# First four tiles in streams of their own, first projections by tile, and two pairs of value products in column tiles

## The chip, the core and the metric

The kernel runs on one core of one Trainium2 chip. The metric is the device time in microseconds (us) of one execution, the median over several. The core has five engines with queues of their own: TensorE (PE) multiplies matrices and loads their stationary operand (PEld), VectorE (DVE) and ScalarE (ACT) work elementwise, GpSimd (POOL) does small things and masks, and SyncE (SP) issues the transfers (DMA). Each engine works its queue off in order; semaphores order the engines against each other.

## The reference

Two layers, each twice with the same weights: attention in four segments with a compressive memory, then a feed-forward block with ReLU. There are 2048 tokens of 640 features, 32 heads of 20, and 1728 hidden features.

```
for s in range(4):                                  # segments of 512 tokens
    p = softmax(q_s k_s^T * scale + causal mask)
    a_dot = p v_s
    a_mem = phi(q_s) M / (phi(q_s) z + 1e-6)
    o_s = g * a_mem + (1 - g) * a_dot               # g = sigmoid(beta)
    M += phi(k_s)^T v_s;  z += sum(phi(k_s))
x = x + (o @ wo);   x = x + relu(layernorm(x) @ w1) @ w2
```

with q, k, v = layernorm(x) @ wq, wk, wv. All inputs are bf16. In the first segment the memory is empty, so only the softmax part counts there.

## The kernel before

Everything stays on chip; x is held in 16 tiles of 128 tokens (`x_sb`). The two attention layers have four segments each. A segment's heads go in 8 groups of four heads, and two groups make a pair m, 32 pairs over the two layers; pairs 0 to 3 are the first segment of the first layer.

The order of the instructions is made by a planner (`Sched`, lines 173 to 374). Each part of the work is a generator, a stream with a priority (`S.add`, from line 1480 on), that yields operations with assumed durations, waits for events (`Need`) and for buffers (`Acq`). The planner always emits the operation that can start first, with the priority deciding ties, and so writes a fixed queue for every engine. Where it foresees a gap of over 300 ns on PE it fills it with small products on a unit matrix (`keep_busy`, line 189; they show as L627). The whole is planned once for each of 32 values of an assumed cost of a change between PE's tile modes (`STARTS`, line 161), and the plan with the smallest end, by the planner's own estimate with random transfer delays, is the one that is built.

PE has three modes here. Full products use all of the 128 x 128 array. The scores (L1103) run four at a time on 20 rows each, one for each head, in row mode. Products of the probabilities with the values (L1246) run four at a time on 32 columns each, in column mode.

The opening: x tiles 0 and 1 are loaded by transfers of their own (`x0a`, `x0b`), tiles 2 and 3 by one (`x01`). Two streams normalize them, `first_ln_a` for tiles 0 and 1 and `first_ln_b` for 2 and 3. DVE makes the statistics (L651, L653), adds epsilon (L661), POOL takes the power -1/2 (L665, or L765 for tiles 2 and 3 together), DVE normalizes into `xn_tok` (L705), PE transposes in five pieces (L728), and DVE or ACT copies the result out to `xnT` (L734, L735). For tile 2 ACT makes the statistics, by a sum and a sum of squares (L753, L757), with small DVE products between. `first_pair` handles two tiles: it sets the event `xt` for the pair when both are copied. `proj_first` then makes the projections to keys (wk) and queries (wq) for segment 0 in groups of five products: 128 output features (c), 256 tokens (the half h), so each group needs both tiles of a half. DVE or ACT writes a group out to `stg` (L816, L817). When both halves of c = 0 are there, SP moves heads from `stg` to `pad` (L913) and the first scores can run. `consts` fills masks on POOL and waits for both halves' `xt` first.

Values: exps (L1155, ACT) write the probabilities `PT`, POOL masks the diagonal blocks (L1167), and `apply(m)` multiplies by the values. There are two forms. By token (`values_by_token`, L1197), the probabilities are the stationary operand and a product has 21 columns, 40 products for a group; DVE divides straight from PSUM into `o_sb` (L1209, L1210, L1213). By column tiles (L1246), the values are stationary, 16 products for a group; DVE or ACT casts the result to `av` (L1254, L1255), SP transposes it by a transfer to `avt` (`turn_av`, L671), and `divide` divides it into `o_sb` (L1282, L1283, L1290). `BY_TOKEN` (line 1179) names segment (0, 0), so pairs 0 to 3 go by token and all others (`LATER`, line 1261) by column tiles.

At a segment's end SP transposes `o_sb` to `oT` (L671), PE projects it with wo, DVE adds it to x (L1317), and a second normalization and the feed-forward block follow. SP's queue also holds the spills of projections to `scr` (L889), the loads of `pad` from there (L934), the turns of `phk` for the memory, and the later loads of weights.

Of the kernel before, what the change touches and what calls it, by code (L numbers as in the profile page):

```python
# [6 lines left out]
dt = mybir.dt  # L7
# [400 lines left out]
def plan(switch, sb, sem_, psum, dram, A_x, A_wq, A_wk, A_wv, A_wo, A_beta, B_x, B_w1, B_w2, out):  # L408
# [248 lines left out]
    def chain(t0, n, tk, sq=None):  # L657

        sl = slice(t0, t0 + n)
        if sq is None:  # L660
            tk = yield dve(n, 1, lambda e: e.tensor_scalar(lnU[:, sl], mv[:, sl, 1], LN_EPS, None, ALU.add), tk)  # L661
# [3 lines left out]
        tk = yield pool(760, lambda e: e.tensor_tensor(rstd[:, sl], lnU[:, sl], mhalf[:, 0:n], ALU.pow), [tk] + h)  # L665
        return tk

    def turn(slot_sem, dst, src, waits):
# [40 lines left out]
    def first_pair(p, tch):  # L709
        idt = yield Need("ident")  # L710
        if p == 0:
            xt = yield Acq(XNT_A)
            xt.users = []
            S.set("xts", 0, 0, tks=[xt])
        else:
            xt = yield Need("xts", 0, 0)
            xt = xt[0]
        bx = yield Acq(XN)
        done = []
        tns = []  # L720
        for k in range(2):
            tn = yield normed(2 * p + k, k, bx, tch[k])
            tns.append(tn)
        for k in range(2):
            t = 2 * p + k
            tn = tns[k]
            pb = lambda bk: bk.ap.bitcast(dt.bfloat16)
            fns = [(lambda e, bk, c=c, k=k: e.transpose(  # L728
                pb(bk)[:, c * 128:(c + 1) * 128], bx.ap[:, k * D + c * 128:k * D + c * 128 + 128], ident[:]),
                c == FC - 1) for c in range(FC)]  # L730
            bk, tT = yield pe((88.0 if p == 0 else 56.0) * FC, fns, [tn] + idt, acq=MISC)
            dst = xt.ap[:, t * FC:(t + 1) * FC, :].rearrange("p c n -> p (c n)")
            src = pb(bk)[:, 0:D]
            tc = yield evac(D, 1.5, lambda e, dst=dst, src=src: e.tensor_copy(dst, src),  # L734
                            lambda e, dst=dst, src=src: e.activation(dst, src, ACT.Copy), [tT])  # L735
            bk.release(tc)
            done.append(tc)
        bx.release(tT)
        S.set("xt", 0, 0, p, tks=done)

    def first_ln_a():
        tch = []
        for t in range(2):
            w = yield Need(("x0a", "x0b")[t])
            tk = yield from stats(t, w)
            tk = yield from chain(t, 1, [tk])
            tch.append(tk)
        yield from first_pair(0, tch)

    def first_ln_b():  # L750
        w = yield Need("x01")
        junk = hT[:, 10:13, :].rearrange("p c n -> p (c n)")[:, 0:D]
        t0 = yield act(D + 350, lambda e: e.activation(  # L753
            junk, x_sb[:, 2, :], ACT.Copy, accum_out=asum[:, 0:1]), w, psum=False)
        tm = yield dve(2, 1, lambda e: e.tensor_scalar(
            mv[:, 2, 0:1], asum[:, 0:1], 1.0 / D, None, ALU.mult), [t0])
        t1 = yield act(D + 470, lambda e: e.activation(  # L757
            junk, x_sb[:, 2, :], ACT.Square, scale=-1.0, bias=mv[:, 2, 0:1],
            accum_out=asum[:, 2:3]), [tm], psum=False)
        t3 = yield from stats(3, w)  # L760
        t1 = yield dve(1, 1, lambda e: e.tensor_scalar(
            lnU[:, 2:3], asum[:, 2:3], 1.0 / D, LN_EPS, ALU.mult, ALU.add), [t1])
        t3 = yield dve(1, 1, lambda e: e.tensor_scalar(lnU[:, 3:4], mv[:, 3, 1:2], LN_EPS, None, ALU.add), [t3])
        h = yield Need("mhalf")
        tch = yield pool(760, lambda e: e.tensor_tensor(  # L765
            rstd[:, 2:4], lnU[:, 2:4], mhalf[:, 0:2], ALU.pow), [t1, t3] + h)
        yield from first_pair(1, [tch, tch])


    def proj_ln(a, s):  # L770
# [27 lines left out]
    def proj_part(a, s, c, n, h):  # L798
# [428 lines left out]
    def apply(m):  # L1227

        a, r = divmod(2 * m, NSEG * G)
        s, g0 = divmod(r, G)  # L1230
        vt = yield Need("v", a, s)
        if (a, s) in BY_TOKEN:
            tk = yield from values_by_token(m, a, s, g0, vt)
            yield from done_values(a, s, g0, tk)
            return
        sl = None
        ev = []
        for z in range(2):
            mk = yield Need("p", 2 * m + z)
            pt, mk = mk[0], mk[1:]  # L1240
            if sl is None:
                sl = yield Acq([AV])
            fns = []
            for j in range(NJ):
                for hh in range(4):
                    fns.append((lambda e, bk, j=j, hh=hh, pt=pt, g=g0 + z: e.matmul(  # L1246
                        bk.ap[32 * hh:32 * hh + wide(g, hh), 128 * j:L],
                        VAUG[vx(a, s)][:, j].rearrange("p h e -> p (h e)")[
                            :, (4 * g + hh) * (DH + 1):(4 * g + hh) * (DH + 1) + wide(g, hh)],
                        pt.ap[:, hh, PT_OFF[j]:PT_OFF[j] + L - 128 * j], start=(j == 0), stop=(j == NJ - 1)),  # L1250
                        j == NJ - 1 and hh == 3))
            bk, tk = yield pe(545.0, fns, mk + vt, acq=MISC, mode="cols")
            pt.release(tk)
            te = yield evac(L, 1, lambda e, sl=sl, z=z, bk=bk: e.tensor_copy(sl.ap[:, z], bk.ap),  # L1254
                            lambda e, sl=sl, z=z, bk=bk: e.activation(sl.ap[:, z], bk.ap, ACT.Copy), [tk] + sl.tks)  # L1255
# [310 lines left out]
```

## Time and profile before

| what | us |
|---|---|
| median of three runs | 566.28 (564.82 to 566.39) |
| the profiled execution | 565.3 |
| its span in the profile | 563.5 |
| PE busy in the span | 556.4 |
| DVE, ACT, POOL busy | 420.1, 404.2, 195.1 |
| first projection on PE starts | 8.88 |
| first scores start | 19.30 |
| first output projection starts | 84.00 |

In the profile a row of the timeline gives the start and the length in us, the engine, the line, the operation, what it writes and reads with shapes, and how many were merged; behind it, in brackets, stands the idle time before it and what ended it. PE's products overlap in the array, so that a single length is longer than the distance from one start to the next; distances between starts are what count for PE. A line ending in "q" (SPq, ACTq) is an engine that issues transfers.

### The profile page before, as it was taken

The numbers are of one execution on the slowest core, as the hardware profiler recorded it, in microseconds if no ns is written. First come the engines' busy times: TensorE is split into PE (matmuls) and PEld (weight loads), VectorE is DVE, ScalarE is ACT, GpSimd is POOL, SyncE is SP. The second block draws the span as 40 slices with busy tenths as digits, with TensorE's granted clock in tenths as the row PEclk, the third lists the DMA queues.
The fourth block names the chain that finished last, engine by engine and source line by source line (L and its number), as shares of the span: only waits on it lengthen the run. The fifth ranks groups of instructions, "written<-read, shape, count | busy, mean of one in ns | idle before, by whom it ended". The sixth has DMA issues, their size and how long they took to land.

```text
span 563.5 us, 12875 instructions
## 1 busy us (share of the span) xinstructions
PE 556.4 (99%) x5219; PEld 305.0 (54%) x5219; DVE 420.1 (75%) x1070; ACT 404.2 (72%) x512; POOL 195.1 (35%) x302
## 2 busy tenths in 40 slices
PE   8999999999999999999999999999999999999998
PEld 7664555445554454645446544555445654665655
DVE  6989789888999689878898997688747964560202
ACT  4789998987788878778986688778878678113140
POOL 4544344333344335444433443035322433110000
PEclk9999999999999999999999999999999999999999
DMA  8695988383474136542375131880326410512101
GB/s 268 120 221 138 238 218 182 74 224 56 97 171 94 44 88 159 118 95 72 92 163 115 27 66 26 193 148 20 67 80 173 109 43 20 116 45 48 47 1 47
DMA packets 130109, 60.93 MB, mean 108 GB/s; under 512 B 108930, under 2 KB 119938, under 8 KB 130050
## 3 DMA queue, kind: packets, MB, share of 16 engines
q1 hardware_dynamic: 129830, 59.85, 45.5%
q8 instruction: 41, 0.67, 0.5%
q10 hardware_dynamic: 220, 0.26, 0.2%
q14 instruction: 18, 0.15, 0.1%
HBM read 20.57 MB, written 12.85 MB: 59 GB/s over the span
## 4 chain that ended last, share of the span: by engine, by line
PE 87%; DVE 8%; DMA 2%; ACT 1%; SPq 1%; issue 0%
PE ps L643 56%; PE ps L640 11%; PE ps L1103 8%; PE ps L1246 6%; DVE stats L651 2%; PE ps L996 2%; PE ps L1197 1%; PE ps L1047 1%; DVE x_sb L1317 1%; PE ps L1394 1%; DMA avt<-av 1%; DVE xn_tok L705 1%; SPq L913 1%; DMA oT<-o_sb 1%; ACT PT L1155 1%; DVE stg L816 1%
## 5 line engine op out<-in xcount | busy, mean ns | idle before, releaser
L1155 ACT ACTIVATE PT<-ps 128x1024 bf16<-128x1024 f32 x320 | 310.0, 1022 | 70.3 <-PE ps L1103 64.6
L1167 POOL TENSOR_SCALAR_AFFINE_SELECT PT<-PT 128x512 bf16<-128x512 bf16 x256 | 166.6, 668 | 268.2 <-ACT PT L1155 267.9
L643 PE MATMUL ps<-w_r,hT 128*128 128x320 bf16 (+2 forms) x768 | 123.0, 299 | 0.0
L643 PE MATMUL ps<-xnT,w_r 128*128 128x512 bf16 x416 | 113.3, 379 | 0.0
L1317 DVE TENSOR_TENSOR x_sb<-x_sb,ps 128x320 bf16<-128x320 bf16 (+1 forms) x128 | 60.3, 479 | 66.7 <-PE ps L643 66.0
L643 PEld LDWEIGHTS ps<-w_r,hT 128*128 128x128 bf16 x768 | 72.4, 98 | 31.9 <-issue 4.4
L1425 ACT ACTIVATE hT<-ps 128x512 bf16<-128x512 f32 x55 | 32.7, 598 | 50.0 <-PE ps L643 49.7
L1103 PE MATMUL ps<-pad 20*128 20x128 bf16 (+3 forms) x1024 | 64.8, 301 | 1.6 <-ACT PT L1155 0.9
L643 PEld LDWEIGHTS ps<-xnT,w_r 128*128 128x128 bf16 x416 | 39.7, 98 | 44.0 <-issue 3.2
L651 DVE BATCH_NORM_STATS2 stats<-x_sb 128x6 f32<-128x320 bf16 x126 | 56.4, 472 | 2.1 <-DMA x_sb<-in_A_x_dram 1.8
L1254 DVE CAST av<-ps 128x512 bf16<-128x512 f32 x53 | 36.2, 684 | 14.8 <-PE ps L1246 14.7
L1103 PEld LDWEIGHTS ps<-pad 20*128 20x128 bf16 x1024 | 18.3, 92 | 52.6 <-ACT PT L1155 25.6
L643 PE MATMUL ps<-wo_r,oT 128*128 128x320 bf16 x256 | 46.1, 299 | 0.0
L1246 PE MATMUL ps<-PT,v_aug 128*32 128x256 bf16 (+5 forms) x896 | 40.7, 302 | 0.0
L1423 DVE TENSOR_SCALAR hT<-ps 128x512 bf16<-128x512 f32 x49 | 33.4, 683 | 9.1 <-PE ps L643 9.0
L640 PE MATMUL ps<-xnT,w_r 128*128 128x512 bf16 x104 | 39.6, 380 | 0.0
L643 PE MATMUL ps<-wv_r,xnT 128*128 128x320 bf16 x192 | 36.7, 300 | 0.0
L643 PE MATMUL ps<-xnT,wk_r 128*128 128x512 bf16 (+1 forms) x140 | 36.1, 349 | 0.0
L643 PE MATMUL ps<-xnT,wq_r 128*128 128x512 bf16 (+1 forms) x140 | 34.9, 349 | 0.0
L665 POOL TENSOR_TENSOR rstd<-lnU,mhalf 128x2 f32<-128x2 f32 (+2 forms) x25 | 20.8, 831 | 38.0 <-DVE lnU L661 34.4
L816 DVE CAST stg<-ps 128x512 bf16<-128x512 f32 (+1 forms) x48 | 29.5, 618 | 3.3 <-PE ps L643 3.2
L1290 DVE TENSOR_TENSOR o_sb<-avt,rden 128x320 bf16<-128x320 bf16 x56 | 30.5, 562 | 0.6
(117 smaller groups left out, 695.8 us busy)
## 6 DMA issues: line engine op xcount, KB each, us to landing
pad<-scr SPq DMA_DIRECT2D x124, 80.0 KB
scr<-stg SPq DMA_DIRECT2D x34, 256.0 KB, 2.9
out_dram<-x_sb SPq DMA_DIRECT2D x15, 160.0 KB, 1.8
w_r<-in_B_w_dram SPq DMA_DIRECT2D x10, 216.0 KB, 4.2
w_r<-in_B_w_dram SPq DMA_DIRECT2D x13, 160.0 KB, 2.8
x_sb<-in_A_x_dram SPq DMA_DIRECT2D x9, 160.0 KB, 2.8
scr<-w_r SPq DMA_DIRECT2D x5, 256.0 KB, 3.6
x_sb<-in_A_x_dram SPq DMA_DIRECT2D x3, 320.0 KB, 7.2
```

Of the source, the lines that this page charges most:

```text
L640: bk, tk = yield pe(mm_ns(n), [(lambda e, bk, a=a, b=b: e.matmul(bk.ap[:, 0:n] if len(b.shape) == 2 else bk.ap[:, 0:n].rearrange("p (i n) ...
L643: tk = yield pe(mm_ns(n), [(lambda e, k=k, a=a, b=b, bk=bk: e.matmul(bk.ap[:, 0:n] if len(b.shape) == 2 else bk.ap[:, 0:n].rearrange("p (i ...
L651: tk = yield dve(320, 1, lambda e, c2=c2: e.bn_stats(stats6[:, t, c2, :], x_sb[:, t, c2 * 320:(c2 + 1) * 320]), xt)
L816: te = yield evac(N, 1, lambda e, sg=sg, bk=bk: e.tensor_copy(sg.ap[:, t0:t0 + N], bk.ap[:, 0:N]), lambda e, sg=sg, bk=bk: e.activation(sg ...
L1103: fns.append([(lambda e, z=z, j=j, hh=hh, N=N, o=o, sl=sl: e.matmul(ps[:, hh, o:o + N], sl.ap[32 * hh:32 * hh + DH, z, 0, 128 * j:128 * j ...
L1155: tx = yield act(1024, lambda e, dst=dst, src=src: e.activation(dst, src, ACT.Exp, scale=SCALE), sc + pw)
L1167: tm = yield pool(600.0, lambda e, reg=reg: e.affine_select(out=reg, in_=reg, pattern=[[0, 4], [1, 128]], compare_op=ALU.is_ge, fill=0.0, ...
L1246: fns.append((lambda e, bk, j=j, hh=hh, pt=pt, g=g0 + z: e.matmul(bk.ap[32 * hh:32 * hh + wide(g, hh), 128 * j:L], VAUG[vx(a, s)][:, j].re ...
L1254: te = yield evac(L, 1, lambda e, sl=sl, z=z, bk=bk: e.tensor_copy(sl.ap[:, z], bk.ap), lambda e, sl=sl, z=z, bk=bk: e.activation(sl.ap[:, ...
L1317: ta = yield dve(n, 1, lambda e: e.tensor_tensor(x_sb[:, t, c0:c0 + n], x_sb[:, t, c0:c0 + n], bk.ap[:, 0:n], ALU.add), [tk] + list(waits) ...
L1423: th = yield evac(512, 1, lambda e, dc=dc, bk=bk: e.tensor_scalar(hT[:, dc, :], bk.ap[:, :], 0.0, None, ALU.max), lambda e, dc=dc, bk=bk: ...
L1425: lambda e, dc=dc, bk=bk: e.activation(hT[:, dc, :], bk.ap[:, :], ACT.Relu), [tk] + HT.tks)
```

## The change

The four first tiles get a stream each, `first_tile(t)`, with priority 1 to 1.6 rather than 5. Tiles 0 and 1 keep their statistics on DVE, tiles 2 and 3 now have both passes on ACT. The operations on DVE that are named in the list `TURN` must be emitted in its order. The transposes use the banks of X and Y instead of the four others. Tiles 0 and 1 each set an event of their own, `xtt`, and `proj_tile` makes the projections of chunks 0 and 1 for one tile, 128 tokens, into a bank that both tiles share; the other half and the other chunks go on as before. `consts` waits as before for both halves. Pairs 0 and 1 go by column tiles, pairs 2 and 3 stay by token. Beside this, the list of assumed costs is longer (48 values), the planner's assumed durations for the power and the first loads are smaller, and all these alter the plan that is chosen.

```diff
-STARTS = [SWITCH_NS + 0.75 * (k - 32 // 2) for k in range(32)]
+STARTS = [SWITCH_NS + 0.75 * (k - 48 // 2) for k in range(48)]
...
-        tk = yield dma(e, sem_("d_" + name), nbytes, fn, waits, lat=2200.0)
+        tk = yield dma(e, sem_("d_" + name), nbytes, fn, waits, lat={"x0a": 1950.0, "x0b": 1950.0, "x01": 1500.0}.get(name, 2200.0))
...
-        tk = yield pool(760, lambda e: e.tensor_tensor(rstd[:, sl], lnU[:, sl], mhalf[:, 0:n], ALU.pow), [tk] + h)
+        tk = yield pool(600, lambda e: e.tensor_tensor(rstd[:, sl], lnU[:, sl], mhalf[:, 0:n], ALU.pow), [tk] + h)
...
+    TURN = ["s0", "s0", "a0", "s1", "l0", "s1", "n0", "m2", "a1", "l1", "m3", "c0", "n1", "l2", "c1"]
+
+    def in_turn(what, op):
+        i = yield from my_turn(what)
+        r = yield op
+        S.set("turn", i, tks=[])
+        return r
+
+    def first_tile(t):
+        p, k = divmod(t, 2)
+        w = yield Need(("x0a", "x0b", "x01", "x01")[t])
+        if p == 0:
...
+        else:
+            junk = hT[:, 10 - 3 * k:13 - 3 * k, :].rearrange("p c n -> p (c n)")[:, 0:D]
+            ta = yield act(D + 350, lambda e: e.activation(
+                junk, x_sb[:, t, :], ACT.Copy, accum_out=asum[:, t:t + 1]), w, psum=False)
+            tm = yield from in_turn("m%d" % t, dve(60, 1, lambda e: e.tensor_scalar(
+                mv[:, t, 0:1], asum[:, t:t + 1], 1.0 / D, None, ALU.mult), [ta]))
...
+        tch = yield pool(560, lambda e: e.tensor_tensor(
+            rstd[:, t:t + 1], lnU[:, t:t + 1], mhalf[:, 0:1], ALU.pow), [tk] + h)
...
+        bk, tT = yield pe((88.0 if t == 0 else 56.0) * FC, fns, [tn] + idt, acq=[X, Y])
...
+            tc = yield from in_turn("c%d" % t, dve(D, 1.5, lambda e: e.tensor_copy(dst, src), [tT], urgent=True))
...
+        S.set("xtt", t, tks=[tc])
...
+    def proj_tile(t, n, c):
...
+        for k in range(FC):
+            mm = lambda e, bk, k=k: e.matmul(
+                bk.ap[:, 128 * t:128 * t + 128], w_r[:, k, c * 128:(c + 1) * 128],
+                xt.ap[:, t * FC + k, :], start=(k == 0), stop=(k == FC - 1))
...
     def proj_first():
-        order = [(c, n, h) for h in range(2) for c in range(2) for n in range(2)]
-        order += [(c, n, h) for c in range(2, FC) for h in range(2) for n in range(2)]
+        for t in range(2):
+            for n in range(2):
+                for c in range(2):
+                    yield from proj_tile(t, n, c)
+        order = [(2, 0, 0)] + [(c, n, 1) for c in range(2) for n in range(2)]
+        order += [x for x in [(c, n, h) for c in range(2, FC) for h in range(2) for n in range(2)] if x != (2, 0, 0)]
...
-    BY_TOKEN = ((0, 0),)
+    BY_TOKEN = (2,3)
...
-        if (a, s) in BY_TOKEN:
+        if m in BY_TOKEN:
...
-    LATER = range(len(BY_TOKEN) * G // 2, NSEG * G)
+    LATER = [m for m in range(NSEG * G) if m not in BY_TOKEN]
...
-    S.add(5, first_ln_a())
-    S.add(5, first_ln_b())
+    for t in range(4):
+        S.add(1 + 0.2 * t, first_tile(t))
```

In `TURN` a letter names an operation and the digit its tile: s is a half of the statistics, a their aggregation, l the addition of epsilon, n the normalization, m the mean from ACT's sum, c the copy out of PSUM.

More of the change, by code (lines that the diff above doesn't have):

```diff
@@ L707, in normed, with my_turn @@
             ALU.subtract, ALU.mult), [tch] + bx.tks, extra=120)
-    def first_pair(p, tch):
+    HALF = {0: [], 1: []}
+    TURN = ["s0", "s0", "a0", "s1", "l0", "s1", "n0", "m2", "a1", "l1", "m3", "c0", "n1", "l2", "c1"]
+    def my_turn(what):
+        k = CALLED.get(what, 0)
+        CALLED[what] = k + 1
+        i = [j for j, w in enumerate(TURN) if w == what][k]
+        if i:
+            yield Need("turn", i - 1)
+        return i
+    CALLED = {}
+    def in_turn(what, op):
[3 more added lines that the diff above has]
+        return r
@@ L714, in first_pair @@
             S.set("xts", 0, 0, tks=[xt])
-        else:
[L716 to L767, printed above, removed]
@@ new lines, in first_tile @@
+        if k == 0:
+            bx = yield Acq(XN)
+            S.set("bx", p, tks=[bx])
+        xt = yield Need("xts", 0, 0)
+        bx = yield Need("bx", p)
+        xt, bx = xt[0], bx[0]
+        if p == 0:
+            tn = yield from in_turn("n%d" % t, normed(t, k, bx, tch))
+        else:
+            tn = yield normed(t, k, bx, tch)
+        pb = lambda bk: bk.ap[:, 0, :].bitcast(dt.bfloat16)
+        fns = [(lambda e, bk, c=c: e.transpose(
+            pb(bk)[:, c * 128:(c + 1) * 128], bx.ap[:, k * D + c * 128:k * D + c * 128 + 128], ident[:]),
+            c == FC - 1) for c in range(FC)]
@@ L770, in proj_ln @@
+        HALF[p].append((t, tT, tc))
+        S.set("xtt", t, tks=[tc])
+        if len(HALF[p]) == 2:
+            bx.release(*[x[1] for x in HALF[p]])
+            S.set("xt", 0, 0, p, tks=[x[2] for x in sorted(HALF[p])])
     def proj_ln(a, s):
```

45 lines of the change are left out of this document (44 added, 1 removed).

## The prediction, made before the changed kernel had run

> **What bounds the kernel now.** I read the page's head first, then the waits of TensorE (PE), then the timeline of the opening on each engine, then the stretch round 80 us where PE runs out of work, then busy times by stretch.
>
> ```profile
> span 563.5 us, 12875 instructions
> PE 556.4 (99%) x5219; PEld 305.0 (54%) x5219; DVE 420.1 (75%) x1070; ACT 404.2 (72%) x512; POOL 195.1 (35%) x302
> PEclk9999999999999999999999999999999999999999
> ```
> ```profile
> PE ps L623 <- POOL mhalf L576: 1.6, 1, 1.6
> PE ps L1103 <- ACT PT L1155: 0.9, 3, 0.4
> PE ps L728 <- DVE xn_tok L705: 0.8, 2, 0.4
> PE ps L1103 <- DMA pad<-stg: 0.6, 1, 0.6
> PE ps L640 <- DVE av L1254: 0.4, 2, 0.2
> ```
>
> PE is busy in 99% of the span at full granted clock, and all its waits are a few us, half of them in the opening. So the time is the sum of what PE does plus little gaps, and an edit counts by what it takes out of PE's own queue or out of those gaps. Part of the busy time is not work: the 43 warm-up products (L623) and 66 fillers (L627) only keep the engine running where the planner foresaw a gap.
>
> **The opening (tiles in streams, projections by tile).**
>
> ```profile
> 1.58 4.28 PE L623 MATMUL ps<-ident 128*128 128x128 bf16 x43 [1.58 <-POOL mhalf L576]
> ...
> 6.61 0.45 PE L728 MATMUL ps<-ident,xn_tok 128*128 128x128 bf16 x5 [0.35 <-DVE xn_tok L705]
> ...
> 8.04 1.00 PE L627 MATMUL ps<-ident 128*128 128x128 bf16 x15
> 8.88 0.27 PE L640 MATMUL ps<-xnT,wk_r 128*128 128x256 bf16 x1
> ...
> 11.62 0.27 PE L640 MATMUL ps<-xnT,wk_r 128*128 128x256 bf16 x1
> ...
> 12.16 0.27 PE L640 MATMUL ps<-xnT,wq_r 128*128 128x256 bf16 x1
> ...
> 19.30 0.40 PE L1103 MATMUL ps<-pad 20*128 20x512 bf16 x4 [0.62 <-DMA pad<-stg]
> ```
> ```profile
> 4.75 0.15 DVE L661 TENSOR_SCALAR lnU<-mv 128x1 f32<-128x1 f32 x1
> 4.83 0.88 DVE L651 BATCH_NORM_STATS2 stats<-x_sb 128x6 f32<-128x320 bf16 x2
> ...
> 6.11 0.44 DVE L705 TENSOR_SCALAR xn_tok<-x_sb,mv,rstd 128x640 bf16<-128x640 bf16 x1
> ...
> 8.24 0.49 DVE L734 COPY xnT<-ps 128x640 bf16<-128x640 bf16 x1 [0.24 <-PE ps L728]
> ...
> 12.78 1.42 DVE L956 TENSOR_SCALAR rtmp<-stg 128x512 bf16<-128x512 bf16 x1 [1.78 <-ACT stg L817]
> 14.12 0.41 DVE L816 CAST stg<-ps 128x256 bf16<-128x256 f32 x1
> ```
> ```profile
> 4.62 0.74 ACT L753 ACTIVATE hT<-x_sb 128x640 bf16<-128x640 bf16 x1 [1.88 <-DMA x_sb<-in_A_x_dram]
> ...
> 6.23 0.83 ACT L757 ACTIVATE hT<-x_sb,mv 128x640 bf16<-128x640 bf16 x1 [0.78 <-DVE mv L755]
> ```
> ```profile
> 5.00 0.56 POOL L665 TENSOR_TENSOR rstd<-lnU,mhalf 128x1 f32<-128x1 f32 x1 [3.42 <-DVE lnU L661]
> ```
>
> Today the first projection waits for both of the first tiles and starts at 8.88. Four groups of 256 columns and four sets of transposes are through when the fifth group starts at 11.62. I replay the written order with these durations.
>
> Tile 0: one half of tile 1's statistics (0.44) goes ahead of l0, which moves from 4.75 to about 5.0; POOL's power (0.56) ends near 5.8; n0 starts at 5.9, not 6.11, because nothing of tile 1 stands before it now. The transposes followed 0.5 behind n0, so 6.4 to 6.85; the copy, now on DVE (0.49, as at 8.24), ends near 7.45; the first projection starts near 7.5, 1.4 earlier than 8.88.
>
> Tile 1 pays: its copy c1 stands on DVE behind l2, l3 and n2, and l3 waits for ACT, which now does both statistics passes of tiles 2 and 3: two of 0.74 from 4.62, two of 0.83 behind them, with reads near 8.3. Then n2 (0.44) and c1 (0.49) end near 9.6. On PE tile 2's transposes stand ahead of tile 1's projections and wait for n2, near 9.1, so all behind them wait too. PE then has tile 0's twenty products with tile 1's transposes from 7.5 to 8.9, tile 2's transposes from 9.1, ten products from 9.6, tile 3's transposes, ten products: the same work is through near 11.05, not 11.62. A 128-wide product takes 0.056 (fifteen fillers from 8.04 to 8.88) and a 256-wide one 0.109 (five from 11.62 to 12.16), so forty for twenty cost +0.06, in this end. I take **-0.55**; the bounds are -0.2 (only n0's 0.2 survives) and -0.9 (c1 and n2 do not queue).
>
> The first scores come next. They waited 0.62 for the pad transfers, which start only when the cast at 14.12 is done, and that stood behind a slow 1.42 on DVE. The built program has the same pair of instructions in the same order, and its two projections for that cast end where they did (11.05 and three groups of 0.545 is 12.7). PE has one group of 0.545 more ahead of the scores and starts 0.55 earlier, so it comes to them at the same time and the 0.62 stays.
>
> **Values of pairs 0 and 1 by column tiles.**
>
> ```profile
> 28.62 1.16 PE L1197 MATMUL ps<-w_r,PT 128*128 128x21 bf16 x40
> 29.64 0.30 PE L640 MATMUL ps<-wv_r,hT 128*128 128x320 bf16 x1
> ...
> 80.34 1.40 PE L627 MATMUL ps<-ident 128*128 128x128 bf16 x22
> ...
> 82.44 0.73 PE L1246 MATMUL ps<-PT,v_aug 128*32 128x512 bf16 x16
> 83.10 0.70 PE L1103 MATMUL ps<-pad 20*128 20x384 bf16 x8
> 84.00 0.31 PE L640 MATMUL ps<-wo_r,oT 128*128 128x320 bf16 x1 [0.21 <-DMA oT<-o_sb]
> ```
>
> From start to next start a group by token takes 29.64 - 28.62 = 1.02, one by column tiles 83.10 - 82.44 = 0.66 with the way out of its mode. Four groups change: 4 x (0.66 - 1.02) = **-1.44**. The bounds are -1.0, if each also pays about 0.1 to get in, and -1.6. Counting the two built programs, matmuls fall from 5219 to 5127 and fillers from 66 to 50, while changes between full, row and column mode rise from 395 to 405. A change costs about 0.1: sixteen column products, four side by side, stream 512 + 384 + 256 + 128 columns, 0.545 at the pace of the five 256-wide ones, and took 0.66. Four of the ten changes are in the 0.66; six are left: **+0.6**, between 0 and +1.0.
>
> The two extra turns of av go through SP, whose queue must hold them:
>
> ```profile
> 41.15 2.25 SPq L532 DMA_DIRECT2D wo_r<-in_A_wo_dram  x2
> 45.88 0.33 SPq L528 DMA_DIRECT2D x_sb<-in_A_x_dram  x1
> ...
> 77.35 2.71 SPq L671 DMA_TRANSPOSE phk<-phs  x1
> 80.10 3.16 SPq L671 DMA_TRANSPOSE oT<-o_sb  x2
> ```
> ```profile
> 78.66 0.48 DVE L1213 TENSOR_TENSOR o_sb<-ps,rden 128x320 bf16<-128x320 f32 x1
> ```
>
> In the built program the first stands behind the second turn of phk and ahead of the four pad transfers of pair 3, which wait with it, as do the loads of wo behind them. A turn holds SP about 1.6 (two oT in 3.16), and SP stands idle from 43.40 to 45.88, so the queue has caught up before the pads matter: nothing, and up to 1.6 if that hole is gone. Pairs 2 and 3 stay by token, so no turn of av comes into the end of the segment. There o_sb is ready at 79.14 but SP is inside a turn of phk until 80.06, and PE burns 28 fillers of 0.056 (1.6 us) until 84.00. In the new order both oT turns stand ahead of that phk. I work out PE's side by the same steps: 0.6 more of work stands before the last by-token group, 0.55 is gained, so o_sb is ready where it was, and up to 0.9 of SP's delay falls away. The filler count there (28 then, 26 now) says that the planner expects nearly the same hole, so I take a third: **-0.3**, between -0.9 and +0.6.
>
> **The rest.** The wider list of 48 switch values, the power's 600 and the load latencies cost nothing on the chip; they let the planner pick another order for all that follows. The waits above that do not belong to the opening come to 1.7 (0.9, 0.4 and two of 0.2 left out above); I take no change in them, between -1.0 (more than half of them gone) and +1.7 (twice as many).
>
> **Sum.** -0.55 - 1.44 + 0.6 - 0.3 = **-1.7**. The profiled execution took 565.3 (span 563.5 and 1.8 round it), so 563.6. The three runs shown have a median of 566.28, 1.0 above it; I centre between the two, 565.8, and say **564.1**.
>
> **Rivals.** *The order after 84 us is better too*: fewer holes with the shorter queue, the opening at its better bound; -1.7 - 0.35 - 0.9 is about -3, so 562.8. For it: 1.7 of waits are there to be won; against it: the built program still puts fifteen fillers behind the first segment, eleven before.
>
> *The gain is swallowed at the end of segment 0*: exps set the pace to 77 us, the saved PE time is only more fillers, and projections pulled forward leave the same work later. Only the six changes and values survive: -0.8, so 565.0. For it: the 28 fillers; against it: work moved ahead is missing later, where PE is full.
>
> *DVE becomes the bound (slower)*:
>
> ```profile
> 40.00:60.00 20.00, 20.00 (x243) 10.18 (x242) 19.93 (x54) 18.32 (x24) 8.68 (x13) 1.00 0.63 154
> ```
> ```profile
> L1254 DVE CAST av<-ps 128x512 bf16<-128x512 f32 x53 | 36.2, 684 | 14.8 <-PE ps L1246 14.7
> L1290 DVE TENSOR_TENSOR o_sb<-avt,rden 128x320 bf16<-128x320 bf16 x56 | 30.5, 562 | 0.6
> ...
> L1282 DVE RECIPROCAL rden<-avt 128x32 f32<-128x32 bf16 x28 | 9.6, 342 | 6.7 <-DMA avt<-av 6.7
> ...
> L1209 DVE RECIPROCAL rden<-ps 128x16 f32<-128x16 f32 x8 | 2.0, 250 | 1.0 <-PE ps L1197 1.0
> ```
>
> DVE (third busy figure) is busy 19.93 of 20 us just where the new work falls. A pair by column tiles costs it 2 x 0.684 + 0.342 + 2 x 0.562 = 2.8, by token 2 x (0.250 + 0.485) = 1.5 (the small products, one or two a pair, left out), so up to +2.7 for two pairs, all four casts being on DVE in the new order. If PSUM banks then come free late, PE idles that 2.7 and cannot use the 1.44: -1.7 + 2.7 + 1.4 = +2.4, so 568.2. It decides once PE's waits on DVE between 40 and 60 us pass about 2. Against it: PE is at 20.00 there, and much of DVE's load is normalization wanted only tens of us later.
>
> *The clock drops in the opening.* PE now has 14 fillers and transposes between 5.7 and 7.5 where it was fed to 8.88. The first 43 products took 4.28, near 0.1 each against 0.056 later, about 3.6 us at the slow pace; a second such stretch would cost half of it, 1.8, so 564.1 + 1.8 = 565.9. Against it: gaps of 0.35 and 0.62 left the clock at full. [...]
>
> **Chances.** A measurement of this kernel tells about 0.3%, 1.7 us, from no change. My sum lies on that bound: forecast 0.46, of which 0.26 beyond it and 0.20 inside. Better order 0.21, faster. Swallowed 0.14 and clock 0.05, same. DVE 0.14, slower. So faster 0.47, same 0.39, slower 0.14. The likeliest case alone runs from 562.6 to 565.6; the range takes in the better order and part of the slower case: 562.0 to 567.2.
>
> **What would show it.** Right: first projection near 7.5, the fifth group near 11.1, first scores still near 19.3 behind a wait for pads; 16 by-column products in 0.66 in pairs 0 and 1; oT issued as soon as o_sb is written; first out-projection near 83. Wrong: PE waits on DVE between 30 and 60 us, a granted clock under 1.0 in the first 15 us, more than 2 us of waits for exps behind 84 us, or a first score past 20.

## The result, and the profile after

The changed kernel took 570.36 us (median of 4 runs, 569.16 to 571.41), the kernel before beside it 566.07: a ratio of 1.0079, 95% interval 1.0054 to 1.0105. It is slower, by 4.3 us (0.8%), where 564.1 was forecast. The profiled execution took 570.56. Some executions of the kernels below, the 571.41 here among them, show a mean granted clock of 0.997 over the span (in the traces, 3.41 us at half rate) and take some 1 to 4 us more; where a median hangs on that, the times at full clock stand beside it.

The head of the page of the changed kernel, to be held against that of before:

```profile
span 568.5 us, 12692 instructions
PE 556.5 (98%) x5126; PEld 302.1 (53%) x5127; DVE 414.8 (73%) x1066; ACT 406.9 (72%) x518; POOL 195.0 (34%) x303
PEclk9999999999999999999999999999999999999999
```

PE's busy time has not moved (556.4 before), the clock is full, and the span is 5.0 longer: PE idles 12.0 us for 7.1. PE's waits in the changed kernel (total, times, longest):

```profile
PE ps L623 <- POOL mhalf L576: 1.6, 1, 1.6
PE ps L640 <- DVE maskg L614: 1.4, 1, 1.4
PE ps L1156 <- ACT PT L1208: 1.3, 5, 0.3
PE ps L640 <- DVE w_r L920: 1.1, 1, 1.1
PE ps L1049 <- DVE av L1307: 0.9, 1, 0.9
PE ps L640 <- DMA hT<-xn_tok: 0.8, 1, 0.8
PE ps L640 <- DVE v_aug L920: 0.8, 1, 0.8
```

Apart from the first, which both kernels have, before had no wait over 0.62 on one place; now five single ones are 0.8 to 1.4 and lie far apart (four places of 0.2 to 0.4 are left out). Busy times by stretch show where (PE is the second figure; the 20 us from 40 stood in the prediction at 20.00, and before had 19.93 from 20 to 40 and 100.00 from 300 to 400):

```profile
20.00:40.00 20.00, 18.08 (x184) 10.90 (x184) 15.06 (x43) 16.17 (x23) 7.36 (x12) 1.00 0.83 169
40.00:60.00 20.00, 19.16 (x164) 8.61 (x163) 19.83 (x50) 18.21 (x26) 8.97 (x13) 1.00 0.93 192
...
300.00:400.00 100.00, 98.54 (x972) 53.40 (x972) 84.21 (x231) 80.34 (x97) 39.10 (x61) 1.00 0.47 88
```

Products overlap, so a wait can also hide in a longer start-to-start distance. So I took from the trace of before the median distance for each pair of neighbouring product shapes and added these up over each kernel's own order; what the execution took beyond that is waiting (an estimate; the slow warm-up, whose products start 0.107 us apart against 0.056 later, is some 1.7 us of the waits before and 2.1 after). Before: 555.0 of steps and 4.4 of waits. After: 553.4 and 10.9. The work on PE did get shorter by 1.6, and 6.5 of new waits more than swallowed it. (Other ways of telling shapes apart give 1.3 to 3.3 less work and 6.3 to 8.2 more waits, so the direction is sure and the parts are good to about 2 us.)

The opening went as forecast. PE's timeline in the changed kernel:

```profile
6.42 0.60 PE L774 MATMUL ps<-ident,xn_tok 128*128 128x128 bf16 x5
6.86 0.55 PE L627 MATMUL ps<-ident 128*128 128x128 bf16 x7
7.61 0.73 PE L857 MATMUL ps<-xnT,wk_r 128*128 128x128 bf16 x10 [0.20 <-DVE xnT L781]
...
10.97 0.27 PE L640 MATMUL ps<-xnT,wk_r 128*128 128x256 bf16 x1
...
19.82 0.28 PE L640 MATMUL ps<-xnT,wq_r 128*128 128x256 bf16 x1 [1.15 <-DVE w_r L920]
20.03 0.40 PE L1156 MATMUL ps<-pad 20*128 20x512 bf16 x4
...
26.79 0.60 PE L643 MATMUL ps<-xnT,wk_r 128*128 128x256 bf16 x4
28.78 0.30 PE L640 MATMUL ps<-wv_r,hT 128*128 128x320 bf16 x1 [1.39 <-DVE maskg L614]
...
53.03 0.73 PE L1299 MATMUL ps<-PT,w_r 128*32 128x512 bf16 x16
53.69 0.61 PE L643 MATMUL ps<-hT,wq_r 128*128 128x512 bf16 x2
...
56.54 0.31 PE L640 MATMUL ps<-wv_r,hT 128*128 128x320 bf16 x1 [0.84 <-DMA hT<-xn_tok]
```

The first projection starts at 7.61 (7.5 forecast), the fifth group at 10.97 (11.05), and sixteen column products take 53.69 - 53.03 = 0.66. Then come the new waits. The first scores start at 20.03, not 19.3: a projection waits 1.15 for a cast of DVE (L920), and DVE's timeline shows why that is late:

```profile
16.08 0.89 DVE L651 BATCH_NORM_STATS2 stats<-x_sb 128x6 f32<-128x320 bf16 x2 [1.45 <-DMA x_sb<-in_A_x_dram]
...
18.32 0.83 DVE L651 BATCH_NORM_STATS2 stats<-x_sb 128x6 f32<-128x320 bf16 x2
19.19 0.21 DVE L653 BATCH_NORM_AGGREGATE mv<-stats 128x2 f32<-128x12 f32 x1
19.32 0.45 DVE L920 CAST w_r<-ps 128x320 bf16<-128x320 f32 x1
```

The cast is queued behind statistics of tiles 4 to 6, and the load of tiles 4 and 5, issued at 6.99, landed at 16.06; before, it was issued at 6.69 and landed at 14.03. At 28.78 the list names a mask of DVE that was done long ago; what ended the wait is the turn of `hT` (a turn is a transpose made by a transfer), issued at 23.88 and landed at 28.65. Before, this turn was issued at 21.75 and landed at 25.36, a us ahead of its product at 26.39. At 56.54 it is the next segment's `hT`.

What held the turn can be seen in the DMA view of the changed kernel from 24.5 to 28.5 us (40 slices of 0.1 us, busy tenths of the DMA engines; q8 is the queue that loads instructions):

```profile
DMA  0000001699999999999997000000000009999999
GB/s 0 0 0 0 0 0 26 133 218 215 215 210 215 192 205 381 212 210 179 108 44 3 0 0 0 8 8 10 8 10 10 10 13 248 289 255 292 289 287 289
...
q8 instruction: 1, 0.02, 1.5%
```

Both rows count a packet in the slice in which it starts. The turn's small packets (1839 of the 1840 packets there are under 512 bytes) start from 25.1 on, all but cease to start at 26.7 and go on at 27.8. The one large packet is an instruction fetch of 16 KB, under way from 26.08 to 27.03. The hole outlasts it by 0.8 us, in which 8 to 13 GB/s move, for some 210 ahead of it; why it does is not shown. The kernel before has the same hole at 26.1 to 27.3 (its fetch runs from 25.43 to 26.54), but its first turn had landed just ahead of it:

```profile
DMA  9899999999999998000000000000699999899999
```

### The profile page after: what moved, and what is told of

It is laid out like the page before. It is cut to its first block, busy times and chain, and to the rows that moved or that the text cites. A ratio compares the mean times of both kernels' runs of the same rounds, so it can differ in the third digit from the quotient of the medians.

```text
span 568.5 us, 12692 instructions
## 1 busy us (share of the span) xinstructions
PE 556.5 (98%) x5126; PEld 302.1 (53%) x5127; DVE 414.8 (73%) x1066; ACT 406.9 (72%) x518; POOL 195.0 (34%) x303
## 4 chain that ended last, share of the span: by engine, by line
PE 73%; DVE 17%; DMA 5%; ACT 2%; SPq 1%; issue 1%; POOL 1%; ACTq 0%
PE ps L643 48%; PE ps L640 9%; PE ps L1156 7%; PE ps L1299 5%; DVE stats L651 2%; DVE x_sb L1370 2%; DMA x_sb<-in_A_x_dram 2%; PE ps L1049 1%; DVE xn_tok L693 1%; ACT PT L1208 1%; DVE stg L839 1%; PE ps L1100 1%; DVE av L1307 1%; DVE rtmp L1009 1%; DMA phk<-phs 1%; DVE o_sb L1343 1%
## 5 line engine op out<-in xcount | busy, mean ns | idle before, releaser
L1156 PE MATMUL ps<-pad 20*128 20x384 bf16 (+3 forms) x1024 | 64.5, 301 | 1.3 <-ACT PT L1208 1.3
L651 DVE BATCH_NORM_STATS2 stats<-x_sb 128x6 f32<-128x320 bf16 x120 | 52.8, 471 | 1.8 <-DMA x_sb<-in_A_x_dram 1.5
L1307 DVE CAST av<-ps 128x512 bf16<-128x512 f32 x55 | 37.6, 683 | 18.4 <-PE ps L1299 18.1
L1476 DVE TENSOR_SCALAR hT<-ps 128x512 bf16<-128x512 f32 x49 | 33.6, 686 | 13.5 <-PE ps L643 12.9
L1299 PE MATMUL ps<-PT,v_aug 128*32 128x128 bf16 (+3 forms) x896 | 40.7, 302 | 0.0
L1343 DVE TENSOR_TENSOR o_sb<-avt,rden 128x320 bf16<-128x320 bf16 x60 | 33.3, 578 | 0.7
L643 PE MATMUL ps<-xnT,wk_r 128*128 128x512 bf16 (+1 forms) x132 | 33.7, 353 | 0.0
L643 PE MATMUL ps<-xnT,wq_r 128*128 128x512 bf16 (+1 forms) x132 | 33.5, 354 | 0.0
L665 POOL TENSOR_TENSOR rstd<-lnU,mhalf 128x2 f32<-128x2 f32 (+1 forms) x23 | 19.1, 833 | 39.9 <-DVE lnU L661 38.9
```

Source lines behind the costliest of these rows:

```text
L643: tk = yield pe(mm_ns(n), [(lambda e, k=k, a=a, b=b, bk=bk: e.matmul(bk.ap[:, 0:n] if len(b.shape) == 2 else bk.ap[:, 0:n].rearrange("p (i ...
L651: tk = yield dve(320, 1, lambda e, c2=c2: e.bn_stats(stats6[:, t, c2, :], x_sb[:, t, c2 * 320:(c2 + 1) * 320]), xt)
L1156: fns.append([(lambda e, z=z, j=j, hh=hh, N=N, o=o, sl=sl: e.matmul(ps[:, hh, o:o + N], sl.ap[32 * hh:32 * hh + DH, z, 0, 128 * j:128 * j ...
L1343: to = yield dve(320, 1, lambda e, dst=dst, src=src, rz=rz: e.tensor_tensor(dst, src, rz, ALU.mult), [tg] + OSB.tks)
L1476: th = yield evac(512, 1, lambda e, dc=dc, bk=bk: e.tensor_scalar(hT[:, dc, :], bk.ap[:, :], 0.0, None, ALU.max), lambda e, dc=dc, bk=bk: ...
```

## The experiments

**The same two kernels once more.** No edit.

> The changed kernel a second time, for its trace. In its first trace the load of x tiles 4 and 5 landed at 16.06 us (14.03 in the kernel before) and DVE, PE and the turns of xnT behind it waited. If that lateness belongs to the kernel or is common, the load lands past 15.5 again, PE waits over 1 us near 18.4 and near 27.1, and the time is 569 to 571.5. If it was chance of that one execution, it lands near 14.0 to 14.5, both waits are mostly gone and the time is 566 to 568. If the new order is bad by itself, the load may land early and the waits near 27, 37, 55, 166, 180 and 339 us stay.

> The kernel before a second time, for its trace. If the landing of x tiles 4 and 5 scatters from one execution to the next, it may land past 15.5 here; if the kernel before stands it, the time stays at 564.8 to 566.4 then, and if it does not, it rises by 2 to 3 us. If the lateness belongs to the changed kernel, it lands at 14.0 to 14.5 here.

The changed kernel took 571.89, the kernel before 565.48, each with its waits at the same places (after: 18.4, 27, 55, 180 and 339 us, where a place is the start of the last product ahead of the wait; the products that waited start at 19.8, 28.8, 56.5, 181.1 and 339.9 in the first trace). The load of tiles 4 and 5 came late again, at 15.71. The waits belong to the built programs, not to chance.

**Each part alone.** The changed kernel with pairs 0 to 3 by token again, and the kernel before with pairs 0 and 1 by column tiles:

```diff
-    BY_TOKEN = (2,3)
+    BY_TOKEN = (0,1,2,3)
```
```diff
-    BY_TOKEN = ((0, 0),)
+    BY_TOKEN = (2,3)
...
-        if (a, s) in BY_TOKEN:
+        if m in BY_TOKEN:
```

> The changed kernel with pairs 0 to 3 all by token: the opening alone, with an order of its own. My prediction priced the opening at -0.55, so 565 to 566. If the four value groups in column tiles load DVE and SP too much, this one is at 565 to 566.5 and values_only at 569 or more. If the opening does the harm, this one is at 569 or more. If each new order draws its own waits, this one falls anywhere from 564 to 571 whatever the parts do.

> The kernel before with only pairs 0 and 1 by column tiles: the values alone, with an order of its own. My prediction priced the values and changes of mode at -0.84, so 565 to 566. If column tiles load DVE and SP too much in the first 60 us, it is at 569 or more with PE waits on DVE between 30 and 60 us. If the opening does the harm, it is at 564.5 to 566. If each new order draws its own waits, anything from 564 to 571.

Measured 570.22 (ratio 1.0070, 1.0053 to 1.0086) and 570.18 (1.0077, 1.0062 to 1.0092). Each half costs what the whole costs, and steps came to 555.5 and 553.6: the waits rose to 9.9 and 11.3 in both. What the parts share is that the planner drew another order.

**Other orders of both kernels.** The planner's list of starts cut to one value, nothing else changed: 85.0 and 108.25 in the kernel before, 100.75 and 83.5 in the changed kernel.

```diff
-STARTS = [SWITCH_NS + 0.75 * (k - 32 // 2) for k in range(32)]
+STARTS = [85.0]
```

> The kernel before with one other switch value (85.0, not the one that its planner chose): the same work in another order, nothing of the change. If every order draws its own waits and the order of the kernel before is a lucky one, this is at 568 to 572, with as many waits on PE as the changed kernel. If the change itself brings the waits, it is at 565 to 567.

> The kernel before with switch value 108.25, a second other order. If orders draw their own waits: 567 to 573, and not the same as before_85. If the change itself brings the waits: 565 to 567.

> The changed kernel with switch value 100.75, another order of the same changed work. If orders draw their own waits: 566 to 572, on average about 1.5 under the orders of the kernel before, since PE's own steps add up to 1.5 less. If the change itself brings the waits: 569 to 572 in every order, with the same waits in the same places.

> The changed kernel with switch value 83.5, a second other order. If orders draw their own waits: 566 to 572, with other waits than after_100. If the change itself brings the waits: 569 to 572.

| kernel, start | us | ratio to before (95%) | steps + waits of PE |
|---|---|---|---|
| before, 85.0 | 567.84 | 1.0035 (1.0015 to 1.0054) | 554.6 + 7.3 |
| before, 108.25 | 570.40 (569.6 at full clock, four of six) | 1.0077 (1.0049 to 1.0104) | 554.2 + 9.1 |
| changed, 100.75 | 572.89 | 1.0101 (1.0068 to 1.0133) | 554.2 + 13.2 |
| changed, 83.5 | 569.15 | 1.0051 (1.0025 to 1.0076) | 555.0 + 7.9 |

Two other orders of the unchanged kernel lose 1.6 and 4.2 us as well (3.4 at full clock). That the orders of the changed kernel would lie 1.5 below those of the kernel before did not come: these two lie 1.9 above on average, with 2.6 and 3.7 us between the two orders of one kernel. So the order built before is a quiet one among its kind, and 4.4 of waits is not what a new order can count on. This does not yet say what makes an order quiet. In the traces the 16 KB fetches number 41 before and 40 after; PE's products and weight loads in the records, 10,438 and 10,253, come to 254.6 and 256.3 for each fetch, about 256. That speaks for fetches of PE's stream, whose moments are set by how many instructions PE has behind it; the next runs put this to the test.

**The same order, the fetches elsewhere.** The first thing PE runs is its warm-up; made of 11 longer or of 75 shorter products in place of 43, with the planner's cost for it unchanged, it puts 64 instructions fewer or more ahead of all that follows. Every queue keeps its order. First 64 fewer, then 64 more:

```diff
-        tk = yield pe(4600.0, [(lambda e: e.matmul(
-            ps[:, 0, 0:128], ident[:], ident[:], start=True, stop=True), k == 42) for k in range(43)], idt)
+        tk = yield pe(4600.0, [(lambda e: e.matmul(
+            ps[:, 0, 0:512].rearrange("p (i n) -> p i n", n=128), ident[:], ident[:][:, None, :].to_broadcast([128, 4, 128]), start=True, stop=True), k == 10) for k in range(11)], idt)
```
```diff
-        tk = yield pe(4600.0, [(lambda e: e.matmul(
-            ps[:, 0, 0:128], ident[:], ident[:], start=True, stop=True), k == 42) for k in range(43)], idt)
+        tk = yield pe(4600.0, [(lambda e, n=n: e.matmul(
+            ps[0:n, 0, 0:n], ident[:, 0:n], ident[:, 0:n], start=True, stop=True), k == 74) for k, n in enumerate([64] * 60 + [128] * 15)], idt)
```

> The changed kernel with every order as it is, but the 43 warm-up products of 128 columns at the start replaced by 11 of 512 columns, so that TensorE's stream is 64 instructions shorter ahead of everything else. In the traces so far an instruction fetch of 16 KB (about 1.1 us on one DMA engine) comes once for about 256 instructions of TensorE, and a DMA transpose that is in flight at that moment lands some 1.5 us late (avt 3.0 for 1.5 us, hT 3.3 to 3.9 for 2.0). Theory F (fetches): with 64 instructions fewer ahead, the fetches fall at about 17.8, 31.4, 44.9, 59.4 us and so on, for 13.6, 26.1, 40.9, 54.6 before; tiles 4 and 5 land near 14 for 16.1, the waits at 18.4 (1.3), 27.1 (1.6), 55.4 (0.9) and 338.7 us (1.0) go, and others of about 1 to 2 us in all come elsewhere: 566 to 568 us. Theory O (the order alone decides, the fetches don't matter): the same waits in the same places, 570.0 to 571.5 us.

> The kernel before with the same edit of the warm-up and every order as it is. Theory F (fetches decide which transposes land late): the fetches move from 12.9, 25.5, 57.1, 65.4, 87.6 us to about 16.7, 28.8, 60.5, 70.2, 90.9; turns of phk near 60 and 80 us and of oT near 82 are hit, those of hT near 25 and of xnT near 88 are not; the waits move, and the time may come out 0 to 2 us above the kernel before: 565.5 to 568. Theory O (the order alone): the same waits (0.65 at 94, 0.51 at 165.7), 566.0 within 0.5 us.

> The changed kernel with every order as it is and 64 instructions of TensorE more ahead (60 warm-up products of 64 columns and 15 of 128 in place of 43 of 128). Theory F: the fetches fall near 10.5, 22.8, 38.6, 51.7, 62.5 us; the wait at 338.7 goes since avt near 335 isn't hit, that at 18.4 goes if tiles 4 and 5 land on time, those at 27 and 55 may stay, as hT is in flight near both: 566.5 to 569.5 us, with the places of the waits changed. Theory O: the same waits in the same places, 570.0 to 571.5.

> The kernel before with every order as it is and 64 instructions of TensorE more ahead. Theory F: the fetches fall near 9.7, 22.4, 31.9, 42.7, 56.3 us and hit the turns of hT near 23 and 55 us, of phk near 32 and of oT near 83, which the kernel before has free; waits of 1 to 1.5 us come at about 26 and 57 us: 567 to 570 us. Theory O: 566.0 within 0.5 us, with the waits where they are.

| | 64 fewer | as built | 64 more |
|---|---|---|---|
| kernel before | 567.37, 1.0006 (0.9989 to 1.0022) | 566.07 | 572.24, 1.0081 (1.0048 to 1.0114); at full clock 569.37 and 570.27 |
| changed kernel | 569.55, 1.0044 (1.0028 to 1.0060) | 570.36, 1.0079 (1.0054 to 1.0105) | 566.99, 1.0011 (0.9994 to 1.0027) |

The column in the middle is from the first measurement; beside these, the kernel before took 566.62. With 64 more, the same order of the kernel before loses 2.8 and 3.7 us in its two executions at full clock and more in the three others, nearly what the change lost, and the same order of the changed one cannot be told from the kernel before. The fetches moved, though not to the expected microsecond: with 64 fewer the first four of the changed kernel came at 13.0, 27.7, 41.2 and 55.7 us (13.5, 26.1, 40.7 and 54.4 as built), with 64 more at 10.7, 20.6, 38.1 and 48.8. The waits moved with them. In the changed kernel with 64 more, no fetch falls on `hT`:

```profile
DMA  9999999999899952799999999999899999999989
```
```profile
PE ps L1156 <- ACT PT L1208: 2.1, 5, 0.9
...
PE ps L1049 <- DVE av L1307: 0.9, 1, 0.9
```
```profile
19.37 0.40 PE L1156 MATMUL ps<-pad 20*128 20x512 bf16 x4 [0.55 <-DMA pad<-stg]
```

(the same 24.5 to 28.5 us, without a hole and without a row of q8; then the waits and the first scores). The waits at 18, 27, 55 and 339 us are gone, 1.2 + 1.4 + 0.8 + 0.8 = 4.2 by the timeline (4.8 by the steps). The median fell by 3.4 and the profiled execution by 2.1 (568.42), so other waits took back the rest. The one near 180 us (L1049) stays, so that one is the order's own. For 339 us the cause is one turn of `avt`, in the changed kernel

```profile
L671 SPq DMA_TRANSPOSE avt<-av x1: 1232/1232/1232, 334.2 to 334.2; - x1
...
DMA to landing us min/median/max: 4.1/4.1/4.1
```

and with 64 more

```profile
L671 SPq DMA_TRANSPOSE avt<-av x1: 1232/1232/1232, 333.1 to 333.1; - x1
...
DMA to landing us min/median/max: 2.7/2.7/2.7
```

the same transfer, 1.4 us sooner where no fetch meets it. The twenty traces together say the same: from issue to landing a turn of `avt` takes a median of 2.73 us where no fetch begins in that time (454 turns) and 4.24 where one does (130), `oT` 3.13 and 4.64, `xnT` 3.58 and 4.64. In the kernel before with 64 more, the fetch now meets the turns of `oT` (slices of 0.2 us from 80; the hole from 85.2 to 86.4), and PE pays in full, where it waited 0.21 before:

```profile
DMA  9999999993329999999899999900000099999999
...
q8 instruction: 1, 0.02, 0.8%
```
```profile
86.73 0.44 PE L640 MATMUL ps<-wo_r,oT 128*128 128x320 bf16 x1 [1.72 <-DMA oT<-o_sb]
```

That product takes 0.44 where such a one took 0.31 before. The windows behind it show why (the third figure from the end is the granted clock):

```profile
87.00:88.00 1.00, 1.00 (x5) 0.57 (x4) 0.00 (x0) 0.42 (x1) 1.00 (x2) 0.50 1.26 276
88.00:89.00 1.00, 1.00 (x5) 0.61 (x4) 0.49 (x1) 0.00 (x0) 0.19 (x1) 0.50 0.77 208
```

From 86.77 PE runs at half rate for 3.41 us, which costs it half of that, 1.7. Two more traces hold such a stretch, also of 3.41 us, and each begins within 2.1 us of the end of a wait of 1.4 to 1.7 us (1.72 here; 1.66 in the values alone with 64 fewer, 1.40 in the kernel with slack and 64 more, both below). Five other waits, of 1.39 to 1.73 us, had none behind them. So half rate came behind three of eight such waits; whether the wait brings it, and what decides it, is not shown.

Not all came as expected. The four waits also went with 64 fewer, but the sum is 569.55, not 566 to 568: a turn of `xnT` near 403 us was hit (PE waits 1.3), and waits at 113 and 143 us came. In before with 64 fewer a turn of `oT` was hit as expected (a wait of 1.0 near 85 us), but the time, 1.0006, does not tell the theories apart. In before with 64 more the wait came at `oT`, the turns of `hT` got by.

**A control, a better start, and the parts again.** The control has 43 warm-up products of other sizes (10 of 256 columns, 20 of 64, 13 of 128), so the fetches stay where they were. The others are the edits above put together: the changed kernel at start 83.5 with 64 more, and each part alone with 64 fewer.

> A control: the changed kernel with every order as it is and its 43 warm-up products made of other sizes (10 of 256 columns, 20 of 64, 13 of 128), the same number of instructions. Theory F (the place of the fetches decides): the fetches stay near 13.6, 26.1, 54.6 us, the waits at 27, 55, 180 and 339 us stay, 569.5 to 571.5 us, ratio near 1.008. Theory W (the other warm-up itself made the kernel with 64 instructions more faster): 566.5 to 568 us.

> The changed kernel with the list of one start, 83.5 (569.2 us, ratio 1.005), and 64 instructions of TensorE more ahead. There the fetches hit hT near 25 and 53 us and oT near 83 and 84 us, and waits of 1.39, 1.38 and 0.74 us followed. Theory F: they move to about 22.7, 51, 81 us by the rate of the other kernels and hit none of these; the three waits go, about 1 us comes elsewhere: 565.5 to 567.5 us, which is at or below the kernel before. Theory O (the order alone): 569 within 0.7 us.

> The kernel with the opening alone (570.2 us, ratio 1.0070), every order as it is, 64 instructions of TensorE fewer ahead. Theory F: the fetch at 25.5 us that held hT (a wait of 1.36) and that near 372 us move off; those waits go, 566 to 568.5 us. Theory P (the part itself costs the 4 us): 570 within 0.7.

> The kernel with the values alone (570.2 us, ratio 1.0077), every order as it is, 64 instructions of TensorE fewer ahead. Theory F: the waits at 84 us (0.91) and 178 us (1.6) go, that at 55 us (1.3) may stay since the fetch then falls at 55.2: 566.5 to 569 us. Theory P: 570 within 0.7.

The control took 569.79 (1.0060, 1.0038 to 1.0082), with the waits where they were, as its list shows; the one at 18 us alone is gone, since tiles 4 and 5 landed at 14.21 this time:

```profile
PE ps L640 <- DVE maskg L614: 1.1, 1, 1.1
PE ps L640 <- DMA hT<-xn_tok: 1.0, 1, 1.0
PE ps L1049 <- DVE av L1307: 0.9, 1, 0.9
PE ps L640 <- DVE v_aug L920: 0.7, 1, 0.7
```

So it is the number of instructions, not the other warm-up. At start 83.5 with 64 more: 567.32 (1.0014, 1.0000 to 1.0028), for 569.15 without; `hT` (2.5 us of waits) and `oT` (0.7) have left its list, as expected. The opening alone with 64 fewer: 568.75 (1.0041, 1.0025 to 1.0057), for 570.22, a little above what was expected: the wait at 26 us went, others of 0.8 and 0.6 came at 82 and 100. The values alone with 64 fewer: 572.23 (1.0104, 1.0075 to 1.0132), a miss. The waits at 84 and 178 us went as expected, but `hT` stayed hit at 55 us (1.7) and `xnT` was hit near 407 (1.0). No execution of it ran at full clock; in the profiled one the half rate begins at 58.7, just behind the wait for `hT`, and costs 1.7. Without that it would be about as fast as without the edit.

**More time for every transpose.** The planner told that a turn lands 1.5 us later, in the changed kernel, and the same with 64 instructions more:

```diff
-                       issue=max(1400.0, 140.0 * n), lat=2000.0, rate=270.0, holds=True)
+                       issue=max(1400.0, 140.0 * n), lat=3500.0, rate=270.0, holds=True)
```

> The changed kernel with the planner told that a transpose lands 1.5 us later than it assumes now (3500 for 2000 ns in turn()), about what a fetch adds; another order comes out. Theory F with slack: few waits for transposes on TensorE even where one is hit, 566 to 568.5 us. Theory O (every new order draws its own waits, slack or not): 568.5 to 572 us.

> The same order with 64 instructions of TensorE more ahead, so that other transposes are hit. Theory F with slack: within 1.5 us of the run beside it (without slack the same shift moved the changed kernel by 3.4 us and the kernel before by 5.6). Theory F where the slack doesn't help: 2 us or more apart.

Measured 565.95 (0.9994, 0.9982 to 1.0005), the best of the changed kernels and not to be told from the kernel before (566.17 beside it), and 568.08 (1.0027, 1.0015 to 1.0038). PE's list of the first begins so and holds no wait for a transposed tile, although turns are late there too where a fetch meets them (from issue to landing `oT` takes up to 5.1 us for a median of 3.5, `avt` 4.7 for 2.7):

```profile
PE ps L623 <- POOL mhalf L576: 1.6, 1, 1.6
PE ps L1156 <- ACT PT L1208: 1.6, 4, 0.7
PE ps L1049 <- DVE stg L1017: 0.6, 1, 0.6
PE ps L1156 <- DMA pad<-stg: 0.5, 1, 0.5
```

By steps and waits it has 554.5 + 5.4. The two are 2.1 us apart, not within 1.5. With 64 more PE has no wait for a transposed tile either; its long one is behind a plain load, that of beta, to which the edit gave no slack:

```profile
24.38 0.23 ACT L602 ACTIVATE gt<-beta_bc 128x32 f32<-128x32 bf16 x1 [1.82 <-DMA beta_bc<-in_A_beta_dram]
```
```profile
25.57 0.39 PE L1156 MATMUL ps<-pad 20*128 20x256 bf16 x4 [1.40 <-ACT PT L1208]
```

A fetch meets this load (8 KB) in all four programs with 64 more, between 20.5 and 21.0 us: from issue to landing it takes 3.9 to 4.1 us there and 2.6 to 3.1 in the sixteen other traces. In each of the four, PE then waits 0.5 to 1.4 us for an exp near 25 us. So a fetch can hold a plain load too, as far as these four show. Whether the slack made the order less touchy cannot be read from one pair: six other shifts that left the order alone moved the time by 0.8 to 3.4 us at full clock. It is one order, so that the slack and not its luck made it good is possible and not shown.

## Why the prediction failed

*The opening (-0.55)*: right. n0 started at 5.92, the first projection at 7.61, the fifth group at 10.97 for 11.62, so -0.65.

*First scores at 19.30 behind the same 0.62 for the pads*: wrong in the kernel as built (20.03, a wait for the cast), since tiles 4 and 5 landed 2 us late. In three kernels of the same order where they landed by 14.4 the scores started at 19.34 to 19.45 behind 0.55 or 0.56 for the pads, as forecast. The prediction had named a first score past 20 as a sign of being wrong. That a fetch near 13.5 us held that load's last share is possible (packets trickle at 7 to 22 GB/s until 16.1), but in the control it came at 13.2 and with 64 fewer at 13.0, and the load was on time; so this cause is not settled.

*Values (-1.44) and the six changes (+0.6)*: 0.66 a group as forecast, and PE's steps fell by 1.6 in all with the fillers saved; the 0.6 alone was not measured.

*Round 80 us (-0.3, first output projection near 83)*: oT was issued at 82.33, as soon as o_sb was written (82.30), as forecast. But o_sb itself was 3.2 us later than before because of the waits ahead (up to 80 us PE is busy 73.8 us, for 77.0 before), and the projection started at 86.90. Nothing of the 0.3 can be seen.

*The rest*: this step failed. "I take no change in them", with bounds of -1.0 and +1.7, was meant for the later waits of PE. The list without the 1.6 at the start holds 7.5 us for 3.1 before, and by the steps the waits rose by 6.5. The bound came from one trace of one order, as if its waits belonged to the kernel; they belong to an order and to where its instruction fetches fall, and both were drawn anew. Of the five long waits as built, those at 27, 55 and 339 us went when the fetches were shifted and stayed in the control, the one at 18 us went where its load was on time, and the one near 180 us stayed throughout. Fourteen programs with the planner's assumptions as they are, but another order or another warm-up, ran beside the two, and their times go from 567.0 to 572.9.

*The rivals*: a better order (562.8) and the gain swallowed (565.0) did not come. DVE as the bound had the right side for the wrong reason: from 40 to 60 us DVE was busy 19.83 for 19.93, PE's only long wait there was for a turn, and the opening alone, which leaves DVE's share of the values as it was, was just as slow. The clock stayed at full behind the warm-up (1.00 in the view from 6.8 to 20 us), with gaps of 0.20 and 1.15 us there; the warm-up's own slow pace held for all of its 43 products, for 34 of them before, which is some 0.4 us. Later in the span, though, half rate followed waits of 1.4 to 1.7 us in three traces.

What stays open: whether the change itself is worth its 1.6 us of work. By draws, the kernel before gives 566.1, 567.4, 567.8, 570.4 and 572.2 (the last two 569.6 and 569.8 at full clock), the changed one 567.0, 567.3, 569.2, 569.6, 570.4 and 572.9, and 566.0 with slack. The scatter of 3 us and more hides it.

## What to carry to other kernels

Where a planner or a scheduler draws the order, an edit changes the draw, and the waits of the present order say little about the next: run a few other orders of the unchanged kernel first, and take their scatter as the bound of "nothing else changes". A transfer that lands just before its result is wanted is a risk, since a fetch of PE's instructions held transposes, and a small load too, by 1 to 1.5 us here; plan it that much earlier. When the same order may be slow or fast, shift its instruction stream by a part of what one fetch brings (64 of about 256 instructions here) before judging the edit.

## What the runs showed of the hardware

PE's stream is fetched in packets of 16 KB, one for 254.6 of its recorded instructions before (41 for 10,438) and 256.3 after (40 for 10,253); they have a queue of their own in the profile (q8). They start a median of 13.2 us apart before and 13.6 after (8.3 to 22.0 in the two traces), and one takes a median of 1.1 us (0.9 to 1.7). PE does not stop for them where its work is at hand: from 300 to 400 us the kernel before has seven, and PE is busy for 100.00 us. The price here is paid by other transfers. Transposes under way all but stood for 1.1 us in the changed kernel (26.7 to 27.8) and for 1.2 in the kernel before (26.1 to 27.3) and in it with 64 more (85.2 to 86.4). The turn of `avt` near 334 us landed 4.1 us after its issue for 2.7, the load of beta 3.9 to 4.1 for 2.6 to 3.1. Why nearly all other packets cease in that time, and go on only 0.8 us after the fetch is through (27.8 for 27.03, and 27.3 for 26.54 before), no run here shows.

PE's clock fell to half for 3.41 us in three traces, each time within 2.1 us of the end of a wait of 1.4 to 1.7 us (1.72, 1.66 and 1.40), and a mean clock of 0.997 over the span is what one such stretch gives (half of 3.41 in 566).

The ten runs of the changed kernel with 64 more lie at two times, 566.4 to 567.1 (six) and 568.1 to 568.7 (four), all at full clock. Which wait makes the 1.5 us was not tried.
